# Walking the moving operands of every second channel step from high to low addresses

## The chip, the core and the metric

The kernel runs on one core of one Trainium2 chip. The metric is device time in microseconds (us): the median of three runs of the kernel before is 732.78 us, and the three lie between 731.84 and 732.80 us. One further execution was taken by the hardware profiler, and its rows are quoted below.

## The reference

Three layers follow each other on a batch of 4 sequences with 448 tokens and 768 channels (1792 tokens in all). Only the last product pair of the third layer is touched by the change.

```python
def _moe2_ref(x, w_tok1, w_tok2, w_ch1, w_ch2):
    xt = x.transpose(0, 2, 1)
    h = np.maximum(xt @ w_tok1, 0.0) @ w_tok2      # token mixing
    u = x + h.transpose(0, 2, 1)
    h2 = np.maximum(u @ w_ch1, 0.0) @ w_ch2        # channel mixing: 768 -> 1536 -> 768
    return (u + h2)

def reference(...):
    attn_out = _attn_ref(...)     # sigmoid attention, 12 heads of 64
    x = attn_out as [4, 448, 768]
    x = _moe_ref(x, ...)          # causal convolution gate, two 768 x 768 products
    return _moe2_ref(x, ...)
```

The inputs are float32 at the reference; the weights arrive at the kernel as 64-bit words, which it decodes itself.

## The kernel before

**Precision.** Each float32 operand of the dense products is kept as a high and a low part (type float32r). A product of two such operands is three matmuls: high weight by high data, low weight by high data, high weight by low data. That is the inner loop over `(0, 0), (1, 0), (0, 1)` in `ch1` and `ch2`.

**Stages.** The first 133 us or so are attention. Until about 377 us the gate layer and token mixing run batch by batch. From then to the end TensorE runs channel mixing, the only stage that the change touches, here called the channel stage.

**Channel stage.** The 1792 tokens are cut into four tiles of 512, 512, 384 and 384 tokens (`TILES`, line 23; index `t`). The 1536 middle channels are cut into 12 steps of 128 (index `fc`). One step of one tile has two products:

- `ch1(t, fc)`, lines 667 to 686: 18 matmuls (6 blocks of input channels, three parts each) add up in one PSUM bank named `psh`. The stationary operand is a 128 x 128 piece of the weights `wch` (or `w`, the same thing in memory reused from an earlier stage), the moving operand is the tile `us`: 128 partitions by 512 or 384 tokens, one token behind the other. Two `psh` banks take turns, so steps with the same parity of `fc` share a bank. Then `split` (lines 85 to 92) makes the two parts of the result `r`: ScalarE (ACT) writes the high part of the positive values (line 86), and VectorE (DVE) reads the same bank and the high part and writes the low part (line 88).
- `ch2(t, fc)`, lines 688 to 703: 18 matmuls (6 output blocks, three parts each) with `r` as the moving operand add to six PSUM banks named `pso`, which stay open over all 12 steps of a tile. After the last step VectorE adds the residual (line 701), and SyncE's queue stores the result (line 703).

**Order.** Lines 778 to 786 write the order out: `ch1` of step n+1 stands ahead of `ch2` of step n. So TensorE does 18 matmuls of a first product, then 18 of the second product of the step before, and so on; two whole blocks of 18 matmuls stand between the end of a step's first product and the reader of its `r` (one block at the last step of all). In the first tile VectorE and ScalarE also decode weights for steps 5 to 11 (lines 106 to 142). There VectorE masks 32-bit words that lie two words apart in memory (`lo, hi = w[:, :, 0], w[:, :, 1]`, line 103; the masks at lines 108 and 115, the joins at lines 118 and 123), and the mask at line 129 reads words that lie side by side.

The very first block, `ch1(0, 0)`, is issued a little earlier than the rest, among the last token-mixing products (line 752).

Of the kernel before, what the change touches and what calls it, by code (L numbers as in the profile page):

```python
# [30 lines left out]
def tile_kernel(ctx, tc, qT, kT, v, w_val, conv_w, w_out, w_tok1, w_tok2, w_ch1, w_ch2, out):  # L31
# [11 lines left out]
    P = 128  # L43
# [26 lines left out]
    def f(ap):  # L70
        return ap.bitcast(F32)
# [9 lines left out]
    const.tile([P, 40], F32, name="pad_l")  # L81
    pad_r = ctx.enter_context(tc.tile_pool(name="pad_r", bufs=1, side="right"))
    pad_r.tile([P, 56], F32, name="pad_r")

    def split(h_out, l_out, src, relu=False):
        nc.scalar.activation(out=h_out, in_=src, func=AF.Relu if relu else AF.Copy)  # L86
        if relu:
            nc.vector.scalar_tensor_tensor(  # L88
                out=l_out, in0=src, scalar=0.0, in1=f(h_out), op0=ALU.max, op1=ALU.subtract
            )  # L90
        else:
            nc.vector.tensor_tensor(out=l_out, in0=src, in1=f(h_out), op=ALU.subtract)
# [81 lines left out]
    def wo_tile():  # L174
        return wts.tile([P, DM], F32R, tag="wo", bufs=2 * KD, name="wo")
# [143 lines left out]
    def dense_steps(b):  # L319
# [87 lines left out]
        if b + 1 == B:  # L407

            outs = pj(1, 0) + pj(1, 1) + tr(0) + pj(1, 2) + tr(1) + pj(1, 3) + tr(2) + pj(1, 4) + pj(1, 5)

            outs = outs[: -len(pj(1, 5))]
            now = pj(1, 5) + t1(0, 0) + t1(0, 1) + tr(3) + tr(4) + tr(5)
            outs += [s + (True,) for s in now] + t2(0) + t2(1) + t2(2)
            return val, outs, t1(1, 0) + t1(1, 1) + [(18, lambda: ch1(0, 0))], t2(3) + t2(4) + t2(5)
# [156 lines left out]
    wch, us_t, acc, r_t = {}, {}, {}, {}  # L571
# [95 lines left out]
    def ch1(t, fc, lo=0, hi=KD):  # L667
        n_t = TILES[t]
        if lo == 0:
            part["ps"] = psc.tile([P, 512], F32, tag="h", bufs=2, name="psh")  # L670
        ps = part["ps"]
        for kk in range(lo, hi):
            for n, (a, c) in enumerate(((0, 0), (1, 0), (0, 1))):
                nc.tensor.matmul(  # L674
                    ps[:, :n_t], wch[fc][0][a][:, kk * P : (kk + 1) * P], us_t[t, kk][:, c, :],
                    start=kk == 0 and n == 0, stop=kk == KD - 1 and n == 2,
                )
        if hi < KD:
            return
        if (t, fc) == (0, 0):  # L680
            r = [wo_tile()[:, :n_t] for _ in range(2)]
        else:
            r = r_b.pop() if r_b else rp["p"].tile([P, 2, W], F32R, tag="r", bufs=2, name="r")
            r = [r[:, c, :n_t] for c in range(2)]
        split(*r, ps[:, :n_t], relu=True)
        r_t[t, fc] = r

# [92 lines left out]
    for n, (t, fc) in enumerate(seq):  # L780
        order.append((ch1, t, fc))
        if fc == KF - 1 and t + 1 < len(TILES):
            order.append((None, t, fc))
        if n:
            order.append((ch2, *seq[n - 1]))
    order.append((ch2, *seq[-1]))
    for fn, t, fc in order:
        if fn is None:
            for j in range(KD):
                del us_t[t, j]  # L790
                prep_load(t + 1, j)
                prep_split(t + 1, j)
        elif (fn, t, fc) != (ch1, 0, 0):
            fn(t, fc)
# [41 lines left out]
```

## Time and profile before

| what | value |
|---|---|
| median of three runs | 732.78 us (731.84 to 732.80) |
| span of the profiled execution, first to last instruction | 729.8 us |
| TensorE matmul busy (PE) | 724.2 us, 99% of the span |
| TensorE weight load busy (PEld) | 594.1 us, 81% |
| VectorE busy (DVE) | 398.9 us, 55% |
| ScalarE busy (ACT) | 256.7 us, 35% |
| mean granted TensorE clock | 1.000 |

How to read it: the times of the runs contain what lies ahead of the first and behind the last instruction, the span does not; the median is 2.95 us above the profiled span, and the profile gives no other time for its own execution. A busy matmul row overlaps its neighbours in the pipeline, so the mean duration of one matmul is not the spacing between two: the spacing is read from the chain of work, which lists how long a block of 18 took from start to start.

### The profile page before, as it was taken

The page shows a single profiled execution, that of the slowest core. Times are in us where ns is not written, and L with a number is a line of the kernel's source. Part 1 is how long each engine was busy: PE and PEld are TensorE (multiplying, and loading weights), DVE is VectorE, ACT ScalarE, POOL GpSimd, SP SyncE. Part 2 cuts the span into 40 slices and gives each one's busy share as a digit, 9 for nine tenths or more (in the row PEclk, how much of TensorE's full clock was granted, in tenths as well). Part 3 has the DMA queues.
Part 4 walks back from the last instruction along what each step waited for, and adds up shares of the span by engine and source line. Part 5 has one row for each costly group of instructions (what it writes and reads, how often), then busy time and mean ns, then how long its engine had stood idle before and what let it go on. Part 6 is the DMA issues. An engine that isn't in the chain of part 4 may idle for free.

```text
span 729.8 us, 10824 instructions
## 1 busy us (share of the span) xinstructions
PE 724.2 (99%) x4360; PEld 594.1 (81%) x4360; DVE 398.9 (55%) x690; ACT 256.7 (35%) x379; POOL 40.2 (6%) x90
## 2 busy tenths in 40 slices
PE   8999999999999999999999999999999999999998
PEld 3344444799999999999998888888888899999997
DVE  1899766489889878965577999320100400040002
ACT  6899888344334333422343434200000200020000
POOL 0001100000111111002012000000000000000000
PEclk9999999999999999999999999999999999999999
DMA  9847997221344232044927453250000610042001
GB/s 298 252 153 236 266 299 234 83 91 47 102 150 147 76 127 101 17 147 131 311 82 227 162 172 127 67 172 0 1 0 1 201 38 0 1 128 67 1 1 65
DMA packets 56737, 87.24 MB, mean 120 GB/s; under 512 B 8032, under 2 KB 48240, under 8 KB 56688
## 3 DMA queue, kind: packets, MB, share of 16 engines
q1 hardware_dynamic: 50352, 62.86, 28.1%
q0 software_dynamic: 5904, 23.23, 9.0%
q8 instruction: 34, 0.56, 0.3%
q10 hardware_dynamic: 432, 0.46, 0.2%
q14 instruction: 15, 0.12, 0.1%
HBM read 66.68 MB, written 19.86 MB: 119 GB/s over the span
## 4 chain that ended last, share of the span: by engine, by line
PE 98%; ACT 1%; DVE 1%; issue 0%; ACTq 0%
PE psd L334 24%; PE psh L674 24%; PE pso L695 24%; PE pss L256 8%; PE psy L271 8%; PE pst L374 4%; PE pst L387 4%; PE pst L357 1%; ACT ga L258 1%; PE psi L718 0%; DVE dec_a L123 0%; DVE w L132 0%; ACT dec_a L111 0%; DVE dec_e L129 0%; DVE ur L701 0%
## 5 line engine op out<-in xcount | busy, mean ns | idle before, releaser
L88 DVE SCALAR_TENSOR_TENSOR r<-psh,r 128x384 fp32r<-128x384 f32 (+1 forms) x47 | 29.3, 623 | 213.4 <-ACT r L86 213.4
L674 PE MATMUL psh<-us,wch 128*128 128x512 f32 (+1 forms) x648 | 135.5, 362 | 0.0
L695 PE MATMUL pso<-r,wch 128*128 128x384 f32 (+1 forms) x630 | 131.1, 361 | 0.0
L674 PEld LDWEIGHTS psh<-us,wch 128*128 128x128 f32 x648 | 117.3, 188 | 12.7
L695 PEld LDWEIGHTS pso<-r,wch 128*128 128x128 f32 x630 | 113.8, 188 | 11.9
L86 ACT ACTIVATE r<-psh 128x384 fp32r<-128x384 f32 (+1 forms) x47 | 25.5, 543 | 230.7 <-PE psh L674 230.6
L334 PE MATMUL psd<-gv,wo 128*128 128x448 f32 x432 | 92.3, 369 | 0.0
L258 ACT ACTIVATE ga<-pss,bias_s 128x896 f32<-128x896 f32 x84 | 83.6, 1005 | 19.0 <-PE pss L256 18.2
L334 PE MATMUL psd<-xs,w 128*128 128x448 f32 x432 | 89.9, 367 | 0.0
L334 PEld LDWEIGHTS psd<-xs,w 128*128 128x128 f32 x432 | 80.9, 188 | 8.2 <-issue 0.7
L334 PEld LDWEIGHTS psd<-gv,wo 128*128 128x128 f32 x432 | 80.2, 188 | 6.6
L256 PE MATMUL pss<-q,k 64*64 64x448 f32 x672 | 78.5, 537 | 1.0 <-ACT ga L258 0.9
L271 PE MATMUL psy<-ga,v 64*64 64x448 f32 x672 | 77.6, 536 | 0.0
L304 DVE SCALAR_TENSOR_TENSOR gate<-xb,cw,gate 128x448 f32<-128x448 f32 x96 | 65.7, 685 | 2.8
L256 PEld LDWEIGHTS pss<-q,k 64*64 64x64 f32 x672 | 26.0, 133 | 39.4 <-issue 29.0
L271 PEld LDWEIGHTS psy<-ga,v 64*64 64x64 f32 x672 | 25.7, 133 | 37.4 <-issue 35.9
L111 ACT ACTIVATE dec_a<-dec_a,exp_b 128x768 int32<-128x768 int32 (+3 forms) x43 | 36.8, 868 | 37.1 <-DVE dec_a L108 37.1
L123 DVE SCALAR_TENSOR_TENSOR dec_a<-raw,dec_a 128x768 int32<-128x768 int32 (+2 forms) x42 | 37.3, 888 | 19.7 <-ACT dec_a L111 19.7
L674 PE MATMUL psh<-us,w 128*128 128x512 f32 (+1 forms) x216 | 45.2, 362 | 0.0
L695 PE MATMUL pso<-r,w 128*128 128x512 f32 (+1 forms) x216 | 45.1, 362 | 0.0
L674 PEld LDWEIGHTS psh<-us,w 128*128 128x128 f32 x216 | 39.1, 188 | 4.3
L695 PEld LDWEIGHTS pso<-r,w 128*128 128x128 f32 x216 | 39.1, 188 | 4.2
(80 smaller groups left out, 648.7 us busy)
## 6 DMA issues: line engine op xcount, KB each, us to landing
raw<-w_ch SPq DMA_DIRECT2D x24, 768.0 KB, 4.4
v<-v SPq DMA_DIRECT2D x24, 224.0 KB, 6.5
uscr<-x2T POOLq DMA_DIRECT2D x24, 224.0 KB, 3.7
q<-qT SPq DMA_DIRECT2D x23, 224.0 KB, 4.3
k<-kT SPq DMA_DIRECT2D x22, 224.0 KB, 4.5
raw<-w_out POOLq DMA_DIRECT2D x6, 768.0 KB, 8.4
wscr<-pre POOLq DMA_DIRECT2D x12, 384.0 KB, 3.6
xscr<-xb SPq DMA_DIRECT2D x18, 224.0 KB, 4.7
```

The lines of the kernel that those rows point to most:

```text
L88: nc.vector.scalar_tensor_tensor(out=l_out, in0=src, scalar=0.0, in1=f(h_out), op0=ALU.max, op1=ALU.subtract)
L111: nc.scalar.activation(out=t["a"], in_=t["a"], func=AF.Relu, scale=8.0, bias=exp_b)
L123: nc.vector.scalar_tensor_tensor(out=t["a"], in0=hi, scalar=-0x80000000, in1=t["a"], op0=ALU.bitwise_and, op1=ALU.bitwise_or)
L256: nc.tensor.matmul(ps[cols, j, :S], k[rows, keys], q[rows], start=True, stop=True)
L258: nc.scalar.activation(out=a, in_=ps[:, :, :S], func=AF.Sigmoid, bias=bias_s, scale=QK_SCALE)
L271: nc.tensor.matmul(y_t[i + h][cols, :S], v_t[i][rows, c, cols], a[rows, j], start=c == 0, stop=c == NB - 1)
L304: nc.vector.scalar_tensor_tensor(out=acc, in0=x[:, t : t + S], scalar=w, in1=acc, op0=ALU.mult, op1=ALU.add)
L334: nc.tensor.matmul(ps[:, :S], w(a, kk), s[:, c, :], start=kk == 0 and n == 0, stop=kk == KD - 1 and n == 2,)
L374: nc.tensor.matmul(ps[:, :HALF], a, x[:, m], start=n == 0, stop=n == len(mm) - 1)
L387: nc.tensor.matmul(ps[:, :S], a, m[:, t, :], start=t == 0 and n == 0, stop=t == KT - 1 and n == 2)
L674: nc.tensor.matmul(ps[:, :n_t], wch[fc][0][a][:, kk * P : (kk + 1) * P], us_t[t, kk][:, c, :], start=kk == 0 and n == 0, stop=kk == KD - 1 ...
L695: nc.tensor.matmul(acc[j][:, :n_t], wch[fc][1][a][:, j * P : (j + 1) * P], r[c], start=fc == 0 and n == 0, stop=fc == KF - 1 and n == 2,)
```

## The change

A helper `back` takes an operand and returns the same elements with the innermost step negated and the start at the last element. In every step with an even `fc` (0, 2, 4, 6, 8, 10) it is applied to

- the moving operand `us` and the output `psh` of all 18 matmuls of `ch1`, so both are walked from the last token's address to the first's and each token still lands in its own column;
- the two parts of `r`, for all who use them: ScalarE and VectorE store token 0 at the highest address and the last token at the lowest, VectorE also reads the high part that way, and the 18 matmuls of `ch2` read `r` from the highest address down. The output `pso` of the second product is written in ascending order as before.

Odd steps are as they were. No instruction of work is added or removed.

```diff
+    def back(w):
+        steps = [list(x) for x in w.ap]
+        step, n = steps[-1]
+        return type(w)(w.tensor, w.offset + step * (n - 1), steps[:-1] + [[-step, n]])
...
         ps = part["ps"]
+        turn = (lambda x: x) if fc % 2 else back
         for kk in range(lo, hi):
             for n, (a, c) in enumerate(((0, 0), (1, 0), (0, 1))):
                 nc.tensor.matmul(
-                    ps[:, :n_t], wch[fc][0][a][:, kk * P : (kk + 1) * P], us_t[t, kk][:, c, :],
+                    turn(ps[:, :n_t]), wch[fc][0][a][:, kk * P : (kk + 1) * P], turn(us_t[t, kk][:, c, :]),
                     start=kk == 0 and n == 0, stop=kk == KD - 1 and n == 2,
                 )
...
             r = [r[:, c, :n_t] for c in range(2)]
+        r = [turn(x) for x in r]
         split(*r, ps[:, :n_t], relu=True)
```

The order of the work is the same on every engine; ScalarE, VectorE, GpSimd and SyncE have the same instructions with the same waits. TensorE gains 20 waits: in the steps 2, 4, 6, 8 and 10 of each tile the first matmul of `ch1` now waits on TensorE's own count (`PE_49`). Here is TensorE's queue before, around the first product of step 6 of the first tile (`psh_4247` is its bank, `pso` the second product of step 4 and then step 5, the numbers behind names count buffers):

```order
L695 MATMUL pso_4064<-r_4186,wch4_3854 128x512 [waits DMASW6_49,Activation_49]
L695 MATMUL pso_4064<-r_4186,wch4_3854 128x512 [waits DMASW7_49]
L695 MATMUL pso_4064<-r_4186,wch4_3854 128x512 [waits DVE_49]
...
L695 MATMUL pso_4084<-r_4186,wch4_3854 128x512 x3
L674 MATMUL psh_4247<-us_3515,wch6_3852 128x512 x3
L674 MATMUL psh_4247<-us_3561,wch6_3852 128x512 x3
...
L674 MATMUL psh_4247<-us_3763,wch6_3852 128x512 x3
L695 MATMUL pso_4064<-r_4226,wch5_3853 128x512 [waits Activation_49]
```

And the same place in the changed kernel:

```order
L702 MATMUL pso_4064<-r_4186,wch4_3854 128x512 [waits DMASW6_49,Activation_49]
L702 MATMUL pso_4064<-r_4186,wch4_3854 128x512 [waits DMASW7_49]
L702 MATMUL pso_4064<-r_4186,wch4_3854 128x512 [waits DVE_49]
...
L702 MATMUL pso_4084<-r_4186,wch4_3854 128x512 x3
L680 MATMUL psh_4247<-us_3515,wch6_3852 128x512 [waits PE_49]
L680 MATMUL psh_4247<-us_3515,wch6_3852 128x512 x2
L680 MATMUL psh_4247<-us_3561,wch6_3852 128x512 x3
...
L680 MATMUL psh_4247<-us_3763,wch6_3852 128x512 x3
L702 MATMUL pso_4064<-r_4226,wch5_3853 128x512 [waits Activation_49]
```

Nothing moved; the first matmul into `psh_4247` carries a wait. What it waits for is the last matmul of step 4 into the same bank, which stands three blocks of 18 matmuls ahead of it.

## Rows read from the trace of the kernel before

**Rows 1.** The page: busy time by engine, share of the span, instructions.
```profile
PE 724.2 (99%) x4360; PEld 594.1 (81%) x4360; DVE 398.9 (55%) x690; ACT 256.7 (35%) x379; POOL 40.2 (6%) x90
...
PEclk9999999999999999999999999999999999999999
```

**Rows 2.** The page: the chain that ended last, by engine and by line.
```profile
PE 98%; ACT 1%; DVE 1%; issue 0%; ACTq 0%
PE psd L334 24%; PE psh L674 24%; PE pso L695 24%; PE pss L256 8%; PE psy L271 8%; PE pst L374 4%; PE pst L387 4%; PE pst L357 1%; ACT ga L258 1%; PE psi L718 0%; DVE dec_a L123 0%; DVE w L132 0%; ACT dec_a L111 0%; DVE dec_e L129 0%; DVE ur L701 0%
```

**Rows 3.** Groups of matmuls of the channel stage: name, count | busy, mean ns | idle.
```profile
L674 PE MATMUL psh<-us,wch 128*128 128x512 f32 (+1 forms) x648 | 135.5, 362 | 0.0
L695 PE MATMUL pso<-r,wch 128*128 128x384 f32 (+1 forms) x630 | 131.1, 361 | 0.0
L674 PE MATMUL psh<-us,w 128*128 128x512 f32 (+1 forms) x216 | 45.2, 362 | 0.0
L695 PE MATMUL pso<-r,w 128*128 128x512 f32 (+1 forms) x216 | 45.1, 362 | 0.0
L695 PE MATMUL pso<-wo,wch 128*128 128x512 f32 x18 | 4.2, 389 | 0.0
```

**Rows 4.** Chain in order of time, channel stage: start, us, block of TensorE.
```profile
564.24 4.08 PE psh L674 x18
568.32 4.08 PE pso L695 x18
...
604.65 3.12 PE psh L674 x18
...
716.97 3.12 PE psh L674 x18
720.09 6.26 PE pso L695 x36
```

**Rows 5.** Windows of the channel stage: busy time per engine, granted clock, DMA share.
```profile
core 0: us, PE busy (x) PEld busy (x) DVE busy (x) ACT busy (x) POOL busy (x), PEclk, DMA share, GB/s
390.00:480.00 90.00, 90.00 (x399) 74.53 (x398) 66.92 (x97) 32.95 (x44) 0.00 (x0) 1.00 0.42 137
480.00:560.00 80.00, 80.00 (x355) 66.24 (x354) 9.73 (x15) 5.39 (x9) 0.00 (x0) 1.00 0.11 35
560.00:640.00 80.00, 80.00 (x440) 77.15 (x439) 14.42 (x25) 9.69 (x19) 0.00 (x0) 1.00 0.17 55
640.00:731.00 91.00, 86.33 (x499) 86.01 (x497) 16.32 (x32) 9.44 (x19) 0.00 (x0) 1.00 0.17 53
```

**Rows 6.** Groups of 380 to 731 us with shapes apart: the split.
```profile
L88 DVE SCALAR_TENSOR_TENSOR r<-psh,r 128x512 fp32r<-128x512 f32 x23 | 15.9, 690 | 88.4 <-ACT r L86 88.4
L86 ACT ACTIVATE r<-psh 128x512 fp32r<-128x512 f32 x23 | 13.7, 594 | 97.4 <-PE psh L674 97.4
L88 DVE SCALAR_TENSOR_TENSOR r<-psh,r 128x384 fp32r<-128x384 f32 x24 | 13.4, 558 | 125.0 <-ACT r L86 125.0
L86 ACT ACTIVATE r<-psh 128x384 fp32r<-128x384 f32 x24 | 11.9, 495 | 133.2 <-PE psh L674 133.2
```

**Rows 7.** Timeline of 712 to 731 us: start, us, instructions merged, idle before.
```profile
713.88 0.49 ACT L86 ACTIVATE r<-psh 128x384 fp32r<-128x384 f32 x1 [5.75 <-PE psh L674]
714.41 0.56 DVE L88 SCALAR_TENSOR_TENSOR r<-psh,r 128x384 fp32r<-128x384 f32 x1 [5.68 <-ACT r L86]
```

**Rows 8.** Groups of 380 to 731 us: decoding, words apart and side by side.
```profile
L129 DVE TENSOR_SCALAR dec_e<-dec_a 128x768 int32<-128x768 int32 x15 | 8.4, 557 | 0.3
L108 DVE TENSOR_SCALAR dec_a<-raw 128x768 int32<-128x768 int32 x14 | 7.8, 556 | 1.0 <-DMA raw<-w_ch 0.8
```

**Rows 9.** Chain in order of time, attention: float32 matmuls on quarter arrays.
```profile
56.88 0.75 PE psy L271 x8
57.63 0.75 PE pss L256 x8
```

**Rows 10.** Weight loads of the channel stage: mean ns of one.
```profile
L674 PEld LDWEIGHTS psh<-us,wch 128*128 128x128 f32 x648 | 117.3, 188 | 12.7
L695 PEld LDWEIGHTS pso<-r,wch 128*128 128x128 f32 x630 | 113.8, 188 | 11.9
```

## The prediction, written before the changed kernel ran

> **What bounds the kernel now.** I read the page's busy times first. TensorE's matmuls fill 724.2 of 729.8 us, at a granted clock of ten tenths in every slice [rows 1]. The chain of work that ended last says the same from the other side: 98% of the span hangs on TensorE, and the two products that the change touches hold 24% each [rows 2]. Then I read the channel stage alone. In the windows from 390 to 640 us the matmuls are busy for the whole of each window, and in the last one only the tail behind 726 us is missing; VectorE falls from 66.92 us in 90 to below 17 us per window, ScalarE from 32.95 to below 10, and the DMA share is 0.42 and then 0.11 to 0.17 [rows 5]. No group of these matmuls has idle time ahead of it [rows 3]. So in this stage time is the number of matmuls times their spacing, and only what alters that spacing can alter the end.
>
> The spacing comes from the chain in order of time. A block of 18 matmuls with 512 columns takes 4.08 us, 226.7 ns each; one with 384 columns takes 3.12 us, 173.3 ns each [rows 4]. [...] All these operands are walked upwards, without gaps. The trace holds no matmul that walks down, so the one thing that matters here, the column rate of a descending walk, it doesn't show.
>
> **What the change touches, in numbers.** Each of the two products has 864 matmuls (648 + 216 and 630 + 216 + 18) [rows 3]. Half of the steps are even, so 432 matmuls of the first product walk both their moving operand and their output downwards, and 432 of the second walk the moving operand downwards alone. Half of each 432 have 512 columns, half 384, a mean of 448: 193,536 columns per product.
>
> **Term 1, the columns of TensorE.** Bounds from both sides. The slow end by the nearest row: the attention matmuls with float32 operands on quarter arrays take 0.75 us for 8 of 448 columns [rows 9]; with four quarters at work that is 0.375 us per 448 columns, 0.84 ns a column, twice 0.417, and the slowest that TensorE moves columns in this trace. At that rate the 432 first products would cost 193,536 x 0.42 = 81 us more, and all 864 reversed matmuls 162 us. These rows are of another element type and not of another direction, so they give the size of a halved rate and no reason for it. The fast end: the 13.3 ns between two matmuls could go, if they came from how the start of one walk follows the end of the one before; 864 x 13.3 = 11.5 us less. I take 0. [...]
>
> **Term 2, the 20 new waits.** Each asks for the last matmul that used the same bank, three blocks of 18 ahead: at least 9.4 us back at 3.12 us a block [rows 4]. It has long been met, and a wait that is met costs nothing visible: the second product's blocks begin with a wait on ScalarE and carry one on VectorE, the first product's mostly have none, and both kinds take 4.08 us, or 3.12 us in the later tiles [rows 4]. Cost 0. Its upper bound: if such a wait kept the next weight load from starting early, each would lay one load bare, 188 ns [rows 10], 20 x 0.188 = 3.8 us.
>
> **Term 3, the split on ScalarE and VectorE.** 24 of the 48 splits write downwards, and VectorE reads one input downwards. A split now takes 0.49 + 0.56 us in the small tiles [rows 7] and 0.594 + 0.690 us in the large ones [rows 6]. The result of step 10 of the last tile is there at 714.41 + 0.56 = 714.97 us, and its reader starts at 720.09 [rows 4, 7]: 5.1 us of cover, two blocks less the split. Were both instructions to take twice as long, 2.1 us in place of 1.05, 4 us of cover would remain. In the first tile VectorE also decodes, up to some 0.75 of the time [rows 5]; there two blocks are 8.16 us against 1.3 us, and a doubled split for six steps adds 6 x 0.69 = 4 us to a VectorE that has 23 us free in that window. The last step, the only one with a single block of cover, is odd and untouched. Cost 0. The residual and the store follow `pso`, which is written as before. The other queues gain nothing: the transfers are the same and none waits for anything new.
>
> **The sum.** 0 + 0 + 0: the span stays at 729.8 us. The median of the runs is 732.78 us, 2.95 us above that span for what lies around it, so I forecast 732.8 us. About 0.2%, 1.5 us, is what a measurement of this kernel can tell from no change.
>
> [...]
>
> **Rivals.**
>
> *The reversed output halves the column rate.* Place: the 432 first products of even steps. [...] A block of 512 columns then takes 18 x (512 x 0.833 + 13.3) = 7.9 us in place of 4.08, one of 384 columns 6.0 us in place of 3.12. It decides from the first column on, since TensorE has no slack to give [rows 5]. Sum: 193,536 x 0.417 = 80.6 us, so 813.4 us. [...] Against it: each bank still gets the same columns, in reversed order, and no row shows a limit of this kind. [...]
>
> *The reversed moving operand halves it.* Then both products of the even steps pay, 864 matmuls: 2 x 80.6 = 161 us, 894 us. Against it: reading by four-byte steps downwards touches the same words in as many accesses, and [rows 8] show an engine that doesn't mind gaps.
>
> *A small price per wait or per matmul.* The 20 waits at their bound give 3.8 us, 736.5 us. A start that is some nanoseconds later for each of 864 reversed matmuls would be of the same order, 864 x 5 ns = 4.3 us. Against it: blocks with and without waits are equal to 0.01 us [rows 4].
>
> *The gap shrinks.* At most 11.5 us, down to 721.3 us. For it: I can't say from rows what the 13.3 ns are. Against: they are the same for 384 and 512 columns, so they belong to the change of matmul and not to the place where the walk starts.
>
> That the change doesn't do what it says is excluded: the built instructions of even steps carry a step of -1 and start at the last element, with the outputs of the first product among them.
>
> **Chances and range.** No change 0.56; reversed output slow 0.18; moving operand slow 0.10; a small price 0.09; a smaller gap 0.07. Nothing in the profile bears on the first two rivals directly, so they keep 0.28 between them. The likeliest case alone gives 731.3 to 734.3 us. The range must leave out no more than 2 in 10: with the likeliest case, the small price and half of the gap's range it holds about 0.7, so it has to reach the slow output; from 727 to 816 us it leaves out the slow moving operand and the lower part of the smaller gap, some 0.14. Faster by over 0.2%: 0.07; within: 0.56; slower: 0.37, the three slower cases.
>
> **What would show it.** In the changed profile the blocks of even and odd steps stand in turn in the chain. If I am right, all take 4.08 or 3.12 us as before. If the output is slow, the even blocks of the first product alone take 7.9 and 6.0 us and the second product keeps its time; if the moving operand is slow, the even blocks of both do. A price of the waits shows as some 0.2 us more in the first product's blocks of steps 2, 4, 6, 8 and 10 and none in step 0. A price of the split shows only in its two groups, which may grow without any idle time on TensorE. I am wrong if any block of the channel stage changes its length, or if the chain leaves TensorE there.

## The result, and the profile after

Three runs of the changed kernel took 737.35, 737.59 and 737.55 us, a median of 737.55 us against 732.78 us before: 4.77 us more, ratio 1.0067 with a 95% interval of 1.0051 to 1.0082. Five further runs on another occasion gave 737.75 us and a ratio of 1.0072 (1.0058 to 1.0086). The change makes the kernel slower by 0.7%: more than the 0.2% that a measurement can tell, and a small part of what a halved column rate would cost.

The page after: busy time by engine, and the granted clock, in the form of [rows 1].

```profile
PE 729.7 (99%) x4360; PEld 596.2 (81%) x4360; DVE 398.7 (54%) x690; ACT 256.5 (35%) x379; POOL 40.1 (5%) x90
...
PEclk9999999999999999999999999999999999999999
```

The span is 735.4 us, 5.6 us longer, and TensorE's busy time grew by 5.5 us at the same number of matmuls and the same clock. So the time didn't go into waiting: the matmuls themselves stand further apart. The chain in order of time shows which (start, us, block of TensorE, as in [rows 4]; here the end of the second tile, with 512 columns, and the beginning of the third, with 384; the marks ... stand for lines left out):

```profile
559.49 4.20 PE psh L680 x18
563.69 4.09 PE pso L702 x18
567.78 4.08 PE psh L680 x18
571.87 4.21 PE pso L702 x18
...
589.71 3.20 PE psh L680 x18
592.91 3.12 PE pso L702 x18
596.03 3.12 PE psh L680 x18
599.15 3.20 PE pso L702 x18
602.36 3.20 PE psh L680 x18
605.56 3.12 PE pso L702 x18
```

Each line is one block of 18 matmuls; `psh` is a first product, `pso` a second product of the step before. The block of the second product at 571.87 belongs to the even step 10 of the second tile and takes 4.21 us, where 4.08 stood before; the odd one ahead of it takes 4.09. In the third tile the blocks of even steps take 3.20 us in place of 3.12, and it makes no difference whether it is the first product, whose output descends too, or the second, whose output doesn't. The odd steps are as they were, but for up to 0.02 us in the first one behind an even block. Per matmul that is 4.20/18 = 233.3 ns against 226.7, 6.7 ns more at 512 columns, and 3.20/18 = 177.8 ns against 173.3, 4.4 ns more at 384.

The sum: 24 blocks of 512 columns at 0.12 us and 24 of 384 at 0.08 us make 4.8 us; with some 0.3 us in the odd blocks behind them it is 5.1 us. The first of the 24 blocks stands alone ahead of the others, among the token mixing. From the start of the first block of the second product to the end of the last the chain has 342.5 us (389.49 to 731.96), where it had 337.5 us before (388.80 to 726.35, [rows 4] for the end): 4.9 us, which is that sum without the first block and rounding. Of the remaining 0.7 us of the longer profiled span, 0.6 us lies ahead of that first block, where the two kernels don't differ, and isn't the change's.

The splits, from the groups of 376 to 740 us with shapes apart, as in [rows 6]:

```profile
L93 DVE SCALAR_TENSOR_TENSOR r<-psh,r 128x512 fp32r<-128x512 f32 x23 | 15.9, 689 | 92.2 <-ACT r L91 92.2
L91 ACT ACTIVATE r<-psh 128x512 fp32r<-128x512 f32 x23 | 13.7, 595 | 101.7 <-PE psh L680 101.6
...
L93 DVE SCALAR_TENSOR_TENSOR r<-psh,r 128x384 fp32r<-128x384 f32 x24 | 13.4, 557 | 127.0 <-ACT r L91 127.0
L91 ACT ACTIVATE r<-psh 128x384 fp32r<-128x384 f32 x24 | 11.8, 492 | 135.3 <-PE psh L680 135.3
```

Means of 689 and 595 ns where 690 and 594 stood, 557 and 492 where 558 and 495 stood: half of these write downwards, and neither ScalarE nor VectorE takes longer for it.

### The profile page after: what moved, and what is told of

It is laid out like the page before. It is cut to its first block, busy times and chain, and to the rows that moved or that the text cites. A ratio compares the mean times of both kernels' runs of the same rounds, so it can differ in the third digit from the quotient of the medians.

```text
span 735.4 us, 10826 instructions
## 1 busy us (share of the span) xinstructions
PE 729.7 (99%) x4360; PEld 596.2 (81%) x4360; DVE 398.7 (54%) x690; ACT 256.5 (35%) x379; POOL 40.1 (5%) x90
## 4 chain that ended last, share of the span: by engine, by line
PE 98%; ACT 1%; DVE 0%; DMA 0%; issue 0%; SPq 0%; ACTq 0%
PE psd L339 24%; PE pso L702 24%; PE psh L680 24%; PE pss L261 8%; PE psy L276 8%; PE pst L379 4%; PE pst L392 4%; PE pst L362 1%; ACT ga L263 1%; DMA k<-kT 0%; DVE dec_a L128 0%; DVE w L137 0%; ACT dec_a L116 0%; DVE dec_e L134 0%; DVE ur L708 0%
## 5 line engine op out<-in xcount | busy, mean ns | idle before, releaser
L680 PE MATMUL psh<-us,wch 128*128 128x512 f32 (+1 forms) x648 | 137.5, 366 | 0.0
L702 PE MATMUL pso<-r,wch 128*128 128x384 f32 (+1 forms) x630 | 133.2, 365 | 0.0
```

Source lines behind the costliest of these rows:

```text
L680: nc.tensor.matmul(turn(ps[:, :n_t]), wch[fc][0][a][:, kk * P : (kk + 1) * P], turn(us_t[t, kk][:, c, :]), start=kk == 0 and n == 0, stop= ...
L702: nc.tensor.matmul(acc[j][:, :n_t], wch[fc][1][a][:, j * P : (j + 1) * P], r[c], start=fc == 0 and n == 0, stop=fc == KF - 1 and n == 2,)
```

## The experiments

**Which part carries the price: one part per tile.**

```diff
-        turn = (lambda x: x) if fc % 2 else back
+        same = lambda x: x
+        even = fc % 2 == 0
+        t_in = back if even and t in (1, 3) else same
+        t_out = back if even and t in (0, 3) else same
+        t_src = back if even and t in (0, 1) else same
+        t_r = back if even and t == 2 else same
...
-                    turn(ps[:, :n_t]), ..., turn(us_t[t, kk][:, c, :]),
+                    t_out(ps[:, :n_t]), ..., t_in(us_t[t, kk][:, c, :]),
...
-        r = [turn(x) for x in r]
-        split(*r, ps[:, :n_t], relu=True)
+        r = [t_r(x) for x in r]
+        split(*r, t_src(ps[:, :n_t]), relu=True)
```

> Even steps only, one part of the change per token tile: tile 0 walks only the output of the first product downwards (the split reads it back downwards), tile 1 only the moving operand of the first product, tile 2 only the moving operand of the second product, tile 3 the first product's moving operand and output together. Theory M (a price per matmul of a descending moving operand, none for the output): tile 0 stays at 4.08 us a block; tile 1 has first-product blocks of 4.20 us; tile 2 second-product blocks of 3.20 us, first 3.12; tile 3 first-product blocks of 3.20 us. Stage 6 x (0.12 + 0.08 + 0.08) = 1.7 us longer than before, some 734.5 us. Rival O (the output carries it in the first product): tile 0 at 4.20 us, tile 1 at 4.08 us. Rival W (the 20 new waits carry it): only blocks with such a wait are longer, and each by one long interval at its first matmul.

Its chain in order of time: first two blocks of tile 0 (only outputs descend; `psh` at 434.07 is an odd step, at 442.23 an even one), then two of tile 1 (only the first product's moving operand descends), then two of tile 2 (only the second product's), and last an even first product of tile 3 (moving operand and output).

```profile
434.07 4.08 PE psh L685 x18
...
442.23 4.08 PE psh L685 x18
...
491.33 4.20 PE psh L685 x18
495.54 4.10 PE pso L707 x18
...
606.06 3.12 PE psh L685 x18
609.18 3.20 PE pso L707 x18
...
675.21 3.20 PE psh L685 x18
```

With only the output descending every block keeps 4.08 us. With only the moving operand descending the even first products of tile 1 take 4.20 us, and in tile 2 the even second products 3.20 us. In tile 3, with moving operand and output together, the even first products take 3.20 us, no more than tile 2's second products with the moving operand alone. One run took 733.99 us against 732.33 us before on that chip, 1.7 us more, as Theory M had it. So in this run the output's direction is free, and the price is the moving operand's: 0.12 us a block of 512 columns and 0.08 us one of 384.

**Every step downwards.** One line: `turn = back`.

> Every step walks downwards, odd ones too. Theory M: all 48 blocks of 512 columns take 4.20 us and all 48 of 384 take 3.20 us, 48 x 0.12 + 48 x 0.08 = 9.6 us more than before, 742.4 us, ratio 1.013. Rival T (the price is that of turning round between steps): no step turns any more, all blocks at 4.08 and 3.12 us, 732.8 us, ratio 1.000.

The median of four runs is 742.0 us, ratio 1.0129 (1.0111 to 1.0147). Two lines of its chain, from the second and from the third tile:

```profile
503.35 4.20 PE psh L680 x18
...
605.54 3.20 PE psh L680 x18
```

All blocks are alike, at 4.20 and 3.20 us; twice the reversed matmuls make twice the time. The price is not that of turning round.

**What in a descending walk costs: other orders of the same columns.** Only the first product's moving operand, even steps.

```diff
-        turn = (lambda x: x) if fc % 2 else back
+        kind = {
+            0: ("words_down", n_t), 2: ("blocks_down", 4), 4: ("words_down", 4),
+            6: ("blocks_down", 16), 8: ("words_down", 16), 10: ("blocks_down", n_t // 2),
+        }.get(fc)
...
-                    turn(ps[:, :n_t]), ..., turn(us_t[t, kk][:, c, :]),
+                    as_walk(ps[:, :n_t], kind), ...,
+                    walk(us_t[t, kk][:, c, :], kind),
...
-        split(*r, ps[:, :n_t], relu=True)
+        split(*(walk(x, kind) for x in r), as_walk(ps[:, :n_t], kind), relu=True)
```

> Moving operand of the first product only, odd steps ascending; even steps each walk in another order: step 0 fully downwards; step 2 groups of 4 words downwards, words within a group upwards; step 4 groups of 4 upwards, words within downwards; step 6 groups of 16 words downwards, words upwards; step 8 groups of 16 upwards, words downwards; step 10 the upper half first, then the lower, both upwards. The split puts each token back, so the result is the same. Theory M1 (what costs is that the walk starts at the upper end and ends at the lower end): steps 0, 2 and 6 at 4.20 us (3.20), steps 4 and 8 at 4.08 us (3.12). Theory M2 (what costs is the order of words that lie side by side): steps 0, 4 and 8 at 4.20 us (3.20) or more, steps 2 and 6 at 4.08 us (3.12). Step 10 at 4.08 us (3.12) by both. Rival D (the second dimension of the walk costs by itself): every even step but 0 is longer, step 10 too.

The chain in tile 1, the first products of steps 2, 4, 6, 8 and 10:

```profile
492.50 4.21 PE psh L697 x18
...
508.96 4.08 PE psh L697 x18
...
525.28 4.20 PE psh L697 x18
...
541.74 4.80 PE psh L697 x18
...
558.82 4.08 PE psh L697 x18
```

Groups of 4 words (16 bytes) downwards with their words upwards cost as much as the full reversal; words downwards inside groups of 4 cost nothing; groups of 16 words downwards cost 0.12 us again. So far M1. But words downwards inside ascending groups of 16 take 4.80 us, six times the price, where M1 has none: both theories fall. At 384 columns the same walk takes 3.60 us, again six times the price of 0.08 us. The two halves in the other order are free (4.08 us), so a second dimension costs nothing by itself.

**Where the size of the group stops mattering.** A line, in the theories here, is a piece of 4 words (16 bytes): the order of the words inside such pieces was free above (4.08 us), their descent was not (4.21 us). The same kernel with the list

```diff
-            0: ("words_down", n_t), 2: ("blocks_down", 4), 4: ("words_down", 4),
-            6: ("blocks_down", 16), 8: ("words_down", 16), 10: ("blocks_down", n_t // 2),
+            0: ("blocks_down", 8), 2: ("blocks_down", 32), 4: ("blocks_down", 64),
+            6: ("blocks_down", 128), 8: ("words_down", 8), 10: ("words_down", 32),
```

> As the run with other walks of the first product's moving operand; even steps now: step 0 groups of 8 words downwards (words upwards), step 2 groups of 32, step 4 groups of 64, step 6 groups of 128, step 8 groups of 8 upwards with the words downwards, step 10 groups of 32 upwards with the words downwards. In the earlier run groups of 4 and of 16 downwards cost 0.12 us a block, halves of 256 nothing, words downwards in groups of 4 nothing, in groups of 16 0.71 us. Theory B (the price belongs to steps backwards from one 64-byte piece to another): groups of 8 cost 0.12 us, groups of 32, 64 and 128 less and less down to 0; words downwards in groups of 8 between 0 and 0.71 us, in groups of 32 some 0.1 us. Theory L2 (every walk whose lines fall costs the same 0.12 us): groups of 8 to 128 all cost 0.12 us.

Steps 2, 4, 6, 8 and 10 of tile 1:

```profile
492.22 4.19 PE psh L697 x18
...
508.66 4.08 PE psh L697 x18
...
524.98 4.08 PE psh L697 x18
...
541.30 4.18 PE psh L697 x18
...
557.75 4.20 PE psh L697 x18
```

Groups of 8 words downwards (step 0, 4.21 us) cost the full price, groups of 32 (128 bytes) still 0.11 us, groups of 64 (256 bytes) and 128 nothing, and the step is sharp. Words downwards in ascending groups of 8 and 32 cost 0.10 and 0.12 us, so groups of 16 stand alone. Theory L2 is out, since these walks fall as well. Theory B holds in kind, with another size: in these runs the price belongs to the order of the 16-byte pieces within 256 bytes, not to steps between 64-byte pieces, and it doesn't fade out with size (4.19 us with groups of 32 words, 4.08 with groups of 64).

**A clash with the weight loads?** The loads run beside the matmuls: from 560 to 640 us of the changed kernel they are busy for 76.33 us, the matmuls for 80.00. Two runs. In one the weights got narrower, so that in tiles 1 and 3 some steps leave out part of the first product:

```diff
+COLS = (128, 96, 64, 32, 128, 64)
...
+                m = COLS[fc // 2] if t % 2 and 0 < 3 * kk + n < 17 else P
...
-                    turn(ps[:, :n_t]), wch[fc][0][a][:, kk * P : (kk + 1) * P], ...
+                    turn(ps[:m, :n_t]), wch[fc][0][a][:, kk * P : kk * P + m], ...
```

> The changed kernel; in tiles 1 (512 columns) and 3 (384) the matmuls of the first product but its first and last hold only 128, 96, 64, 32, 128 and 64 weight columns in the six step pairs, so those steps leave out part of the sum for the other output channels. Theory C (clash with the weight loads): the price of descending blocks falls with the number of weight columns, from 0.12 us (0.08) to near 0 at 32, and the 13.3 ns between ascending matmuls may fall with it, down to 512 x 0.417 x 18 = 3.84 us (2.88) a block. Theory L (moving reads alone): descending first-product blocks stay 0.12 us (0.08 us) above ascending ones for every number of weight columns.

Tile 1: the first products of steps 2 and 3 (96 columns of weights), 4 and 5 (64), 6 and 7 (32); behind them steps 6 and 7 of tile 3 (384 columns of the moving operand, 32 of weights); and the loads, from the groups of 480 to 580 us:

```profile
493.24 4.20 PE psh L682 x18
...
501.54 4.14 PE psh L682 x18
...
509.88 4.20 PE psh L682 x18
...
518.18 4.14 PE psh L682 x18
...
526.52 4.20 PE psh L682 x18
...
534.82 4.17 PE psh L682 x18
...
691.22 3.16 PE psh L682 x18
...
697.52 3.13 PE psh L682 x18
```

```profile
L682 PEld LDWEIGHTS psh<-us,wch 128*128 128x128 f32 x68 | 12.6, 188 | 2.6
...
L682 PEld LDWEIGHTS psh<-us,wch 128*32 128x32 f32 x32 | 3.5, 108 | 3.8
```

The loads shrink from 188 to 108 ns, and at 512 columns the descending blocks, at 4.20 us, don't gain a hundredth of a microsecond. The ascending ones get slower, from 4.08 to 4.17 us. At 384 columns the descending blocks do fall, from 3.20 us to 3.17 with 64 and 3.16 with 32 columns of weights, where the ascending ones take 3.12 and 3.13 us. That is neither theory: C wanted the descending blocks to fall at both lengths, L wanted a constant distance of 0.12 and 0.08 us. At 512 columns the time of a descending block doesn't hang on the length of the weight loads; at 384 about half of its price goes with them, as C had it in kind. The run doesn't tell the loads from the output, which shrinks to as many partitions as there are weight columns.

In the other run the second product's moving operand starts some words later in its buffer:

```diff
+SHIFT = {2: (0, 4, 8, 16, 32, 64), 3: (2, 12, 24, 48, 96, 128)}
...
+            off = SHIFT.get(t, [0] * 6)[fc // 2]
+            r = [r[:, c, off : off + n_t] for c in range(2)]
```

> The changed kernel; in the last two tiles (384 columns) the result of the split, the moving operand of the second product, is laid some words further along in its buffer: by 0, 4, 8, 16, 32, 64 words in the step pairs of tile 2 and by 2, 12, 24, 48, 96, 128 words in those of tile 3, the same for the even (descending) and the odd (ascending) step of a pair. Theory C (the price is a clash of the moving reads with the weight loads that run beside them, so it hangs on where the two streams stand to each other): second-product blocks of descending steps differ with the shift, some at 3.12 us, some above 3.20; ascending ones may rise too. Theory L (a price of the order of the lines in the moving reads alone): descending blocks 3.20 us and ascending ones 3.12 us at every shift. Rival E (16-byte alignment of the start): only shifts that are no multiple of 4 words (2) differ.

The second products of tile 2: steps 2 and 3 (4 words further), 4 and 5 (8), 6 and 7 (16).

```profile
599.19 3.24 PE pso L704 x18
...
605.62 3.16 PE pso L704 x18
...
611.91 3.23 PE pso L704 x18
...
618.34 3.18 PE pso L704 x18
...
624.67 3.18 PE pso L704 x18
...
631.04 3.12 PE pso L704 x18
```

Ascending blocks rise to 3.16 and 3.18 us at 4 and 8 words, are back at 3.12 at 16 and take 3.15 at 32; descending ones lie between 3.17 us (12 and 48 words) and 3.24 us. At 2 and at 24 words, in tile 3, both directions take the same, 3.23 and 3.18 us: there the descending walk has no price of its own. At 64 and at 128 words both are as without a shift. So the start within 64 words sets the spacing of ascending walks too, and the price of a descending one was measured for buffers that begin at a multiple of 64 words, as every moving operand of the channel stage does in the built kernel. This speaks against L, which had one value for each direction, and against E, since multiples of 4 words differ. It fits C, but since the other run does so at 384 columns only, the clash stays open.

**Other lengths.** `TILES = (496, 480, 416, 400)` with the same buffers (`W = 512`).

> The changed kernel with token tiles of 496, 480, 416 and 400 in place of 512, 512, 384 and 384; odd steps ascend, even ones descend. Theory A (a fixed price per matmul, 6.7 ns as at 512 columns): even blocks 0.12 us longer than odd ones at each length. Theory B (a price per column, 6.67/512 = 0.013 ns): 0.116, 0.113, 0.098 and 0.094 us longer. Theory Q (spacings settle on multiples of 16 columns, 6.67 ns, and the descending walk needs a little more than the ascending one): the difference is not smooth in the length, near 0.12 us at some and below 0.08 us at others. Ascending blocks by 18 x (columns x 0.417 + 13.3 ns): 3.96, 3.84, 3.36 and 3.24 us.

At 480 columns (tile 1; first products of an odd and an even step) and at 400 (tile 3):

```profile
529.63 3.90 PE psh L680 x18
...
537.50 3.96 PE psh L680 x18
```

```profile
697.28 3.24 PE psh L680 x18
...
703.80 3.28 PE psh L680 x18
```

Descending minus ascending is 0.12 us at 512. At 496 the ascending blocks differ among themselves: some take 3.96 us, others 4.01 to 4.03, and the descending ones 4.08, so it is 0.12 us in some steps and about 0.06 in the others. It is 0.06 at 480, 0.05 at 416 (3.44 against 3.39), 0.04 at 400, and 0.08 at 384. That is not smooth, so neither a fixed price (A) nor one per column (B). Of Q, the price varies as it said. An ascending block of 480 columns has a mean of 216.7 ns, 32.5 steps of 6.67 ns, and the trace's single records show what the mean hides: its matmuls start 220 and 213 ns apart in turn, 33 and 32 such steps. At 496, though, descending ones start 224 and 229 ns apart in turn, and the ascending ones of step 3 223, 227, 222 and 221 ns, and no such step gives these. So Q isn't shown and isn't refuted.

**The price taken away.** The walk still goes from the end of the tile to its beginning, but in groups of 64 tokens with the tokens of a group upwards, in both products, the output and the split:

```diff
-        return type(w)(w.tensor, w.offset + step * (n - 1), steps[:-1] + [[-step, n]])
+        return type(w)(w.tensor, w.offset + n - 64, steps[:-1] + [[-64, n // 64], [step, 64]])
```

> The changed kernel, but in even steps the walk goes from the last group of 64 tokens to the first with the tokens of a group upwards, for all operands that the change turns round: moving operands of both products, the first product's output, both parts of the split's result. Theory 256 (the price belongs to the order of the pieces within 256 bytes of the moving operand): no price is left, all blocks 4.08 and 3.12 us, 732.8 us, ratio 1.000, though the walk still runs from the end of the tile to its beginning and all waits of the changed kernel are there. Rival S (the price belongs to the second product or to the split as much, or needs both products turned): even blocks stay above 4.08 and 3.12 us, up to 737.5 us, ratio 1.0065.

The median is 732.29 us, ratio 0.9998 (0.9989 to 1.0007). Its chain: in the second tile the first product of step 11 and the second product of step 10, in the third tile the first product of step 4 and the second product of step 3, so that the second and the third line are blocks of even steps:

```profile
564.59 4.08 PE psh L683 x18
568.67 4.08 PE pso L705 x18
...
598.76 3.12 PE psh L683 x18
601.88 3.12 PE pso L705 x18
```

All of the loss is gone, with the 20 waits of the changed kernel in place. So the waits, and the direction in which the tile is walked from group to group, cost nothing, and the whole of the loss hangs on the order within 256 bytes. The changed kernel ran beside it:

> The changed kernel itself on the same chip beside it, for the size of its price with a narrower interval: ratio 1.0065, 737.5 us, even blocks 4.20 and 3.20 us.

It gave 737.75 us, ratio 1.0072 (1.0058 to 1.0086), as expected. No version ran faster than the kernel before; the nearest thing to it is this one, which ties.

## Why the prediction was right or wrong

The forecast was no change, 732.8 us; the kernel is slower, by the rival with 9 in 100. That 737.55 us lies inside the range of 727 to 816 us is luck: the range reached so far up for the sake of a slow output, and the output is free (4.08 us a block with it alone descending).

- **What bounds the kernel: right.** TensorE has no slack in the channel stage (after the change its matmuls are busy for 90.00 of 90 us from 390 us on, then twice for 80.00 of 80), so the 4.4 to 6.7 ns of each reversed matmul reached the end in full.
- **Term 1, "I take 0": this is the step that failed.** No run shows the 0; they show 6.7 ns for each of 432 matmuls of 512 columns and 4.4 ns for each of 432 of 384, 4.8 us. The bounds held, but their middle was empty: I chose between a full rate and a half. The rate and the gap in them follow from two blocks of [rows 4]: (4.08 - 3.12)/18 us over 128 columns is 0.417 ns a column, and of 4.08/18 us 512 such columns leave 13.3 ns. The one row that I had for 0 was VectorE's [rows 8]: 556 ns over words two apart and 557 over neighbours show nothing of how TensorE reads. In the runs words downwards within 16 bytes are free (4.08 us a block), but the order matters over 256 bytes (4.19 us with groups of 32 words downwards). The small price per matmul, which I had set at 5 ns for 864 matmuls, was the right rival in place and size, and its 4.3 us is 0.5 us short of the blocks' sum. But the 5 ns came from no row, so the size is luck, and the picture behind it, a later start of each walk, isn't what the runs show: the walk in groups of 64 starts near the upper end too and is free (4.08 us), and the one with words downwards in ascending groups of 16 starts near the lower end and costs six times as much (4.80 us).
- **Term 2, the waits, 0: right.** The run by groups of 64 keeps all of them at ratio 0.9998, the run with other orders has none of them and its groups of 4 words pay the full price, and in the changed kernel the second product pays as much as the first and has no new wait. So the half of the small-price rival that put 3.8 us on the waits was wrong.
- **Term 3, the split, 0: right.** Its groups didn't grow, and TensorE never waited for it.
- **Reversed output slow: wrong.** No run shows the halved rate behind its 813.4 us: alone it costs nothing, 4.08 us a block where that rival had 7.9.
- **Moving operand at half rate: the right place, the wrong size.** Both products pay, as that rival said, but 4.8 us and not 161 us. Between 384 and 512 columns a descending matmul takes (233.3 - 177.8)/128 = 0.43 ns a column, where an ascending one takes 0.417, and the whole extra is 3% of a matmul. Whether it sits in the columns or between the matmuls is open.
- **The gap shrinks: wrong.** That the 13.3 ns are the same for 384 and 512 columns was read as a sign that they belong to the change of matmul; at 480 columns the same sum, 216.7 - 480 x 0.417, gives 16.7 ns, and at 384 columns a start 8 words further on adds 3.3 ns to an ascending one (3.18/18 against 3.12/18), so the place where the walk starts has a part in them.

## What to carry to other kernels

In this kernel, where TensorE is busy for 99% of the span, the order in which a matmul walks its moving operand is part of its price: in buffers that begin at a multiple of 256 bytes, no order was faster than float32r words ascending within 256 bytes (4.08 us a block of 512 columns), and pieces of 256 bytes and more could be taken downwards at the same 4.08 us. Why 256 bytes is open; a clash with the weight loads that run beside the matmuls is neither shown nor excluded. Look at the blocks of the chain rather than at busy shares: a few nanoseconds per matmul don't show in a share of 99%, but in 4.20 against 4.08 us. And when a trace doesn't show a walk, a row of another engine is no ground for its price; leave some of the chance between "free" and "half speed".

## What the runs showed of the hardware that was not expected

- Words downwards in ascending groups of 16 cost 0.72 us a block of 18 matmuls (4.80 against 4.08 us), six times as much as the full reversal (0.12 us), in groups of 8 and 32 they cost 0.10 and 0.12 us, in groups of 4 nothing. Why 64 bytes is so much worse is open.
- An ascending moving operand that starts 4 or 8 words further on costs 0.04 to 0.06 us a block of 384 columns (3.16 and 3.18 against 3.12), 2 words 0.11 us, 32 words 0.03 us, 16 or 64 words nothing. At 2 and 24 words ascending and descending blocks take the same time.
- At 512 columns fewer weight columns per matmul made ascending matmuls slower (4.17 against 4.08 us a block at 32), though each load is shorter (108 against 188 ns); at 384 columns it made descending ones faster (3.16 against 3.20 us).
- A descending output in PSUM was free (4.08 us a block with and without), and so were descending writes of ScalarE and VectorE (595 and 689 ns a piece, where 594 and 690 stood).
